# Modulation columns by halves, normalised rows on VectorE, a longer attention tail and separate buffers ahead of w3 in a memory-attention and MLP kernel

## The chip, the cores and the metric

The kernel runs on one core of one Trainium2 chip. The metric is the device time of one execution in microseconds (us). A comparison always uses runs of the kernel before on the same chip in the same rounds. "Ratio" below is the mean time of one kernel's fast runs over the mean of the other's of the same rounds, with a 95% interval; it is therefore not quite the ratio of the medians quoted beside it. Most experiments were timed in other rounds than the changed kernel, so a comparison with the changed kernel goes by the two ratios to the kernel before, or by medians where that is said, and is less certain. The engines are named as the profile names them: PE (TensorE matmuls), DVE (VectorE), ACT (ScalarE), POOL (GpSimd), SP (SyncE).

## The reference, cut to what matters

```python
mod = (silu(c) @ w_mod).reshape(1, 6, 1, 1024)          # sa, ca, ga, sb, cb, gb
h = layernorm(x) * (1 + ca) + sa                        # x: 1 x 2048 x 1024
x = x + ga * A(h, mem0, Wq, Wk, Wv, Wo, 32)   # 64 segments of 32 rows, 32 heads of 128,
                                              # 8 memory rows handed from segment to segment
h = layernorm(x) * (1 + cb) + sb
x = x + gb * B(h, w1, w2, w3, w4)
# B: h = gelu(layernorm(h0) @ w1); four column groups shifted by -1, +1, -2, +2 rows, then @ w2
#    x1 = h0 + that;  return x1 + gelu(layernorm(x1) @ w3) @ w4      (w3: 1024 -> 3584)
```

The stages that matter are, in order of time: the **opening** (modulation, first layer norm, first projections, to some 60 us), the **attention** (to some 760 us), the product with Wo (from 760 us), and the **passage** from w2 to w3 near 1100 us.

## The kernel before: the parts concerned

Opening. The weights of the modulation arrive in four pieces of 1 MB. Both vectors are written only when all four are in. The normalised tile `xn` is written by POOL.

```python
for q in range(4):
    wm = gchunk([P, KT, 512])
    last_wm = nc.sync.dma_start(wm[:], wslice(w_mod, q * 512, 512))
    wms.append(wm)
# ... (cut)
for half in range(2):
    for j in range(KT):
        for kt in range(KT):
            nc.tensor.matmul(pm[:, half * KT + j:half * KT + j + 1], lhsT=wms[half * 2 + j // 4][...], rhs=scT[:, kt:kt + 1], ...)
nc.vector.tensor_copy(saT[:], pm[:, 0:KT])
nc.vector.tensor_scalar(ca1T[:], pm[:, KT:2 * KT], 1.0, None, ALU.add)
# ... for each row tile (cut):
nc.vector.tensor_scalar(nm[:], mean, -1.0, None, ALU.mult)
nc.gpsimd.tensor_tensor(nmr[:], nm[:], rstd, ALU.mult)
nc.gpsimd.tensor_scalar(xn[:], xt[:], rstd, nmr[:], ALU.mult, ALU.add)
# then: transposes and segment sums of xn on PE; hh = xn^T * ca1T + saT
```

Attention. Heads are worked off between the projections of later heads; a tail of 1.55 heads is kept for afterwards.

```python
done, ahead = 0, len(att) - int(len(att) * 1.55 / H)
```

Passage. In w2 each row tile `t` goes through PE, then DVE (`x1b`, with a row sum), ACT (`Square`), POOL (three small instructions), ACT again (`Identity`, which writes the normalised `z`), and a DMA transposes `z` into z2a (tiles 0 to 7) or z2b (tiles 8 to 15). w3 is computed by a scheme with fewer products, which needs sums of z2a (`zs`) and of the weights (`ring`). For w3 a PSUM bank is copied by ACT (`snap`), added to another by DVE (`join`) and passed through gelu by ACT (`hq`).

```python
tp = LT2.enter_context(tc.tile_pool(name="x2_t", bufs=4))     # u2, x1b and z
# ... w2, tile t (cut):
    if i == 10:
        zu = z_sums(0) + w3_sums(0)
    if i >= 10:
        for f in zu[2 * (i - 10):2 * (i - 9)]:
            keep_order(f())
# ... then, over the memory that w2's pools have left (cut):
stm = RF.enter_context(tc.tile_pool(name="x3_sm", bufs=4, side="right"))    # the joins
# ...
def join(a, f, q, bank, s):
    t = stm.tile([P, 512], F32, name="join")
    nc.vector.tensor_tensor(t[:], st[q][bank][:], st[q][s][:], ALU.add)
    gelu(a, f, q, t)
```

## Time and profile before

| | kernel before |
|---|---|
| time, median of 4 runs | 1481.55 us (1480.31 to 1482.04) |
| span of the profiled execution, mean granted clock | 1480.2 us, 0.995 |
| PE busy | 1419.7 us, 96% |
| first projection on PE | 25.18 us |
| PE waits for the transposed V | 6.1 us |
| end of w2's last matmul, first matmul of w3 | 1116.91, 1119.07 us |

PE bounds this kernel, so it is read from PE's gaps: a change that removes no matmul can win only there, or where the granted clock is low. The prediction below shows the lines for that. Two further lines of the timeline of ACT in the kernel before; the columns are start, duration, engine, line and operation, and in brackets the idle time before it with what ended it.

```profile
1125.33 0.19 ACT L1147 ACTIVATION_READ_ACCUMULATOR z<-x1b,ln_nm 128x1 f32 x1
1126.72 1.24 ACT L1154 ACTIVATE z<-x1b,ln_nmr,ln_rstd 128x1024 bf16<-128x1024 f32 x1 [0.74 <-POOL ln_nmr L1153]
```

This is the last row tile of w2. ACT finishes its last normalise at 1127.96 us, 11.05 us after PE ended w2.

### The profile page before, as it was taken

How to read it: one execution, taken by the hardware profiler on the slowest of the kernel's cores; microseconds unless marked ns; L12 is line 12 of the kernel's file. 1: busy time of each engine (PE TensorE's matmuls, PEld its weight loads, DVE VectorE, ACT ScalarE, POOL GpSimd, SP SyncE). 2: the span in 40 equal slices, each digit the busy share in tenths (PEclk: the TensorE clock that was granted, in tenths of full speed). 3: DMA queues.
4: the chain of work that ended last, by engine and by line, in shares of the span. 5: the costliest groups of instructions: out<-in, count | busy, mean ns of one | idle time of the engine just before them, and what ended most of it. 6: DMA issues, size and time to landing. Idle time of an engine off the chain costs nothing.

```text
span 1480.2 us, 24704 instructions
## 1 busy us (share of the span) xinstructions
PE 1419.7 (96%) x9198; PEld 751.7 (51%) x9254; DVE 885.5 (60%) x1943; ACT 683.0 (46%) x1439; POOL 365.3 (25%) x526
## 2 busy tenths in 40 slices
PE   5999999999999999999998999999997999999998
PEld 3575555555565555555554444444443444444443
DVE  5526676777677777666652345345254657576684
ACT  2726666655665666665551122024465661046400
POOL 8411100000000001000001313213023653545625
PEclk9999999999999999999999999999998999999999
DMA  9678877787767887767579999985499783478812
GB/s 324 213 265 188 195 150 170 185 190 155 177 156 175 175 185 171 159 158 178 117 197 314 361 307 368 321 192 157 139 272 247 233 278 111 126 241 252 283 40 78
DMA packets 404149, 303.48 MB, mean 205 GB/s; under 512 B 199082, under 2 KB 356778, under 8 KB 402226
## 3 DMA queue, kind: packets, MB, share of 16 engines
q1 hardware_dynamic: 365904, 242.06, 61.7%
q10 hardware_dynamic: 29330, 30.89, 6.9%
q0 software_dynamic: 8784, 28.85, 6.6%
q8 instruction: 74, 1.21, 0.3%
q14 instruction: 57, 0.47, 0.1%
HBM read 200.56 MB, written 50.63 MB: 170 GB/s over the span
## 4 chain that ended last, share of the span: by engine, by line
PE 77%; DMA 7%; DVE 5%; ACT 4%; issue 4%; POOL 3%; ACTq 0%; SPq 0%; DVEq 0%; POOLq 0%
PE acc L620 30%; PE acc L902 7%; PE bank_b L1291 7%; PE bank_b L1240 6%; PE acc L1069 4%; PE acc L328 3%; PE bank_d L1240 3%; PE acc L318 3%; PE bank_e L1291 2%; PE bank_d L1291 2%; PE acc L1167 2%; PE ps_o L731 2%; PE ps_s L714 2%; PE bank_e L1240 1%; DMA V<-VT 1%
## 5 line engine op out<-in xcount | busy, mean ns | idle before, releaser
L902 PE MATMUL acc<-wstream,OTc 128*128 128x512 bf16 x940 | 207.8, 379 | 6.6 <-DMA OTc<-OTx_d 2.5
L620 PEld LDWEIGHTS <-T 128*128 128x128 f16 x1408 | 130.5, 97 | 119.6 <-issue 2.0
L588 ACT COPY snap<-acc 128x480 f32<-128x480 f32 x264 | 146.0, 564 | 89.2 <-PE acc L620 82.2
L620 PE MATMUL acc<-hh,T 128*128 128x480 bf16 (+1 forms) x704 | 163.1, 366 | 0.3 <-DVE VT L592 0.3
L620 PE MATMUL acc<-hs,T 128*128 128x480 f16 x704 | 157.1, 366 | 0.7 <-ACT snap L588 0.6
L902 PEld LDWEIGHTS <-OTc 128*128 128x128 bf16 x960 | 93.2, 98 | 117.7 <-issue 3.5
L1240 PEld LDWEIGHTS <-ring 128*128 128x128 f16 (+1 forms) x784 | 77.4, 99 | 109.7 <-issue 19.9
L756 POOL DMA_DIRECT2D OTx_d<-OT x32 | 24.9, 777 | 434.4 <-DMA OT<-O 341.6
L718 ACT ACTIVATE E<-ps_s 99x495 bf16<-99x495 f32 (+2 forms) x160 | 87.3, 546 | 48.2 <-PE ps_s L714 47.7
L620 PE MATMUL acc<-hh,wq 128*128 128x480 bf16 x464 | 103.9, 366 | 0.0
L738 DVE TENSOR_TENSOR O<-ps_o,rin_all 99x384 bf16<-99x384 f32 (+1 forms) x192 | 97.1, 509 | 3.8
L1205 ACT COPY snap<-bank_b 128x512 f32<-128x512 f32 x72 | 41.8, 586 | 105.6 <-PE bank_b L1291 58.2
L1291 PEld LDWEIGHTS <-hq 128*128 128x128 bf16 (+1 forms) x560 | 54.7, 98 | 66.1
L731 PE MATMUL ps_o<-V,E 99*128 99x129 bf16 (+1 forms) x704 | 79.7, 220 | 8.7 <-DMA V<-VT 6.1
L592 DVE TENSOR_TENSOR KT<-acc,snap 128x480 bf16<-128x480 f32 x116 | 74.9, 655 | 21.3 <-PE acc L620 18.9
L1095 DVE TENSOR_TENSOR ring<-ring 128x1024 f16<-128x1024 bf16 (+1 forms) x64 | 79.5, 1262 | 5.7 <-PE bank_b L1291 5.3
L731 PEld LDWEIGHTS <-E 99*128 99x128 bf16 (+1 forms) x704 | 56.2, 98 | 46.3 <-issue 8.8
L1010 ACT ACTIVATE u<-x,ln_nmr,ln_rstd 128x1024 bf16<-128x1024 f32 x16 | 19.7, 1231 | 127.0 <-DVE ln_nmr L1009 72.2
L720 DVE TENSOR_TENSOR E<-E,maskB 99x495 bf16<-99x495 bf16 (+1 forms) x128 | 48.1, 376 | 49.7 <-ACT E L718 47.7
L1244 ACT ACTIVATE hq<-join 128x512 bf16<-128x512 f32 x84 | 52.8, 630 | 47.0 <-DVE join L1248 47.0
L1291 PE MATMUL bank_b<-ring,hq 128*128 128x512 f16 (+1 forms) x334 | 73.1, 379 | 0.1
L592 DVE TENSOR_TENSOR VT<-acc,snap 128x480 bf16<-128x480 f32 x90 | 58.0, 651 | 24.9 <-PE acc L620 20.4
(242 smaller groups left out, 2509.5 us busy)
## 6 DMA issues: line engine op xcount, KB each, us to landing
wstream<-in_A_Wo_dram SPq DMA_DIRECT2D x31, 1024.0 KB, 11.1
OTx_d<-OT POOLq DMA_DIRECT2D x32, 512.0 KB, 7.2
wstream<-in_B_w_dram SPq DMA_DIRECT2D x28, 512.0 KB, 5.4
OTc<-OTx_d SPq DMA_DIRECT2D x14, 1024.0 KB, 8.7
ring<-in_B_w_dram SPq DMA_DIRECT2D x28, 512.0 KB, 6.5
ring<-in_B_w_dram SPq DMA_DIRECT2D x8, 1792.0 KB, 10.4
wq<-in_A_Wq_dram SPq DMA_DIRECT2D x16, 512.0 KB, 5.3
wk<-in_A_Wk_dram SPq DMA_DIRECT2D x16, 512.0 KB, 7.3
```

The costliest lines, as they stand in the source:

```text
L588: nc.scalar.copy(t[:], st[q][bank][:, 0:CH])
L592: nc.vector.tensor_tensor(view(d, i), chunks(st[q][bank]), chunks(st[q][s_]), ALU.add)
L620: nc.tensor.matmul(acc[:, 0:CH], lhsT=B[:, k, :], rhs=A[:, k, :], start=(j in (1, 2, 5) and k == 0), stop=(k == 3), skip_group_check=True)
L718: nc.scalar.activation(E[:rows, 0:o], ps[:rows, 0:o], ACT.Exp, scale=DH ** -0.5)
L731: nc.tensor.matmul(ps[:, i, :], lhsT=state["e", h, t // 5][:k, c:c + P], rhs=V[:k, t, 0:DH + 1], start=True, stop=True)
L738: nc.vector.tensor_tensor(O[:rows, ts[0]:ts[0] + n, :], ps[:rows, 0:n, 0:DH], rin[:, :, None].to_broadcast([rows, n, DH]), ALU.mult)
L902: mm = nc.tensor.matmul(accs[tt][:], lhsT=ot[hl // 4][:, hl % 4, tt * P:(tt + 1) * P], rhs=woc[hl // 4][:, hl % 4, :], start=(h == 0), sto ...
L1069: nc.tensor.matmul(acc[:], lhsT=w1s[:, kt, ct * P:(ct + 1) * P], rhs=zT[:, kt, b * 512:(b + 1) * 512], start=(kt == 0), stop=(kt == KT - 1))
L1095: return nc.vector.tensor_tensor(dst, a, b, op)
L1240: nc.tensor.matmul(acc[:], lhsT=B[:, k, q * P:(q + 1) * P], rhs=A[:, k, :], start=(start and k == 0), stop=(k == 3), skip_group_check=True)
L1244: nc.scalar.activation(hq[a][f][:, g * 2 + q, :], src[:], ACT.Gelu_apprx_tanh)
L1291: nc.tensor.matmul(acc[:], lhsT=L3[:, k, i * P:(i + 1) * P], rhs=R3[:, k, :], start=(start and k == 0), stop=(k == 13), skip_group_check=True)
```

## The change

It has four intentions: let the first rows be normalised and modulated before all modulation weights are in; take the normalised tile off POOL; give the attention more distance from its projections; and let w3 start without waiting for the last transposes of w2. The diff, cut to its core:

```diff
-            last_wm = nc.sync.dma_start(wm[:], wslice(w_mod, q * 512, 512))
+            last_wm = nc.sync.dma_start(wm[:], wslice(w_mod, q % 2 * D + q // 2 * 512, 512))
...
-        nc.vector.tensor_copy(saT[:], pm[:, 0:KT])
-        nc.vector.tensor_scalar(ca1T[:], pm[:, KT:2 * KT], 1.0, None, ALU.add)
+            cols = slice(q // 2 * 4, q // 2 * 4 + 4)
+            if q % 2:
+                nc.vector.tensor_scalar(ca1T[:, cols], pm[:, KT + cols.start:KT + cols.stop], 1.0, None, ALU.add)
+            else:
+                nc.vector.tensor_copy(saT[:, cols], pm[:, cols])
...
-                    nc.gpsimd.tensor_tensor(nmr[:], nm[:], rstd, ALU.mult)
-                    nc.gpsimd.tensor_scalar(xn[:], xt[:], rstd, nmr[:], ALU.mult, ALU.add)
+                    nc.vector.tensor_scalar(xn[:], xt[:], mean, rstd, ALU.subtract, ALU.mult)
...
-        done, ahead = 0, len(att) - int(len(att) * 1.55 / H)
+        done, ahead = 0, len(att) - int(len(att) * 1.75 / H)
...
+        tz = LT2.enter_context(tc.tile_pool(name="x2_z", bufs=4))
         tp = LT2.enter_context(tc.tile_pool(name="x2_t", bufs=4))
+        tu = LT2.enter_context(tc.tile_pool(name="x2_u", bufs=3))
...
-            if i == 10:
-                zu = z_sums(0) + w3_sums(0)
-            if i >= 10:
-                for f in zu[2 * (i - 10):2 * (i - 9)]:
-                    keep_order(f())
+            if i == 6:
+                zu = w3_sums(0) + [lambda: None] + z_sums(0)
+            if 6 <= i < 14 and i != 9:
+                keep_order(zu[i - 6]())
...
-        stm = RF.enter_context(tc.tile_pool(name="x3_sm", bufs=4, side="right"))
+        stm = RF.enter_context(tc.tile_pool(name="x3_sm", bufs=3, side="right"))
```

More of the change, by code (lines that the diff above doesn't have):

```diff
@@ L385, in first_pass @@
         pm = small_ps[:, 0:2 * KT]
-        for half in range(2):
-            for j in range(KT):
+        for q in range(4):
+            for j in range(4):
+                col = q % 2 * KT + q // 2 * 4 + j
                 for kt in range(KT):
-                    nc.tensor.matmul(pm[:, half * KT + j:half * KT + j + 1], lhsT=wms[half * 2 + j // 4][:, kt, (j % 4) * P:(j % 4 + 1) * P], rhs=scT[:, kt:kt + 1],
-                                     start=(kt == 0), stop=(kt == KT - 1))
-        nc.vector.tensor_copy(saT[:], pm[:, 0:KT])
-        nc.vector.tensor_scalar(ca1T[:], pm[:, KT:2 * KT], 1.0, None, ALU.add)
+                    nc.tensor.matmul(pm[:, col:col + 1], lhsT=wms[q][:, kt, j * P:(j + 1) * P], rhs=scT[:, kt:kt + 1], start=(kt == 0), stop=(kt == KT - 1))
+            cols = slice(q // 2 * 4, q // 2 * 4 + 4)
[3 more added lines that the diff above has]
+                nc.vector.tensor_copy(saT[:, cols], pm[:, cols])
         hsum = ps1.tile([P, KT, NSEG], F32, name="small_ps")
@@ L413, in f @@
                     mean, rstd = layernorm_stats(sm, xt[:])
-                    nm = sm.tile([P, 1], F32, name="ln_nm")
-                    nc.vector.tensor_scalar(nm[:], mean, -1.0, None, ALU.mult)
-                    nmr = sm.tile([P, 1], F32, name="ln_nmr")
-                    nc.gpsimd.tensor_tensor(nmr[:], nm[:], rstd, ALU.mult)
                     xn = xnp.tile([P, D], BF16, name="xn")
-                    nc.gpsimd.tensor_scalar(xn[:], xt[:], rstd, nmr[:], ALU.mult, ALU.add)
+                    nc.vector.tensor_scalar(xn[:], xt[:], mean, rstd, ALU.subtract, ALU.mult)
                     if t + 8 < NTT:
@@ L1158, in f @@
                 ts = slice(t * P, (t + 1) * P)
-                u = tp.tile([P, D], BF16, name="u2")
+                u = tu.tile([P, D], BF16, name="u2")
                 nc.sync.dma_start(u[:], u_d[ts, :])
@@ L1170, in f @@
                 nc.scalar.dma_start(x1b_d[ts, :], x1b[:])
-                zs[t] = z = tp.tile([P, D], BF16, name="z")
+                zs[t] = z = tz.tile([P, D], BF16, name="z")
                 ln_sums(bsm, z[:], x1b[:], sums)
```

## The prediction

> **What bounds the kernel now.** I read the page first, then the table of stretches of 20 us, then the waits of PE, then the timelines of single engines where PE had gaps.
>
> ```profile
> PE 1419.7 (96%) x9198; PEld 751.7 (51%) x9254; DVE 885.5 (60%) x1943; ACT 683.0 (46%) x1439; POOL 365.3 (25%) x526
> ```
>
> PE is busy for 1419.7 of 1480.2 us, so at most 60.5 us of gaps can be won, plus whatever PE runs at a low clock. The change removes no matmul. Its worth is therefore read only from the stretches in which PE has gaps.
>
> ```profile
> 0.00:20.00 20.00, 7.03 (x162) 6.43 (x163) 7.19 (x31) 1.46 (x2) 15.71 (x50) 1.00 0.97 320
> 20.00:40.00 20.00, 15.16 (x150) 8.77 (x149) 13.91 (x48) 9.86 (x21) 16.92 (x34) 1.00 1.04 338
> 700.00:720.00 20.00, 17.52 (x127) 10.04 (x126) 13.12 (x37) 11.17 (x26) 0.68 (x3) 1.00 0.68 121
> 1100.00:1120.00 20.00, 17.73 (x82) 7.93 (x83) 14.89 (x41) 10.63 (x15) 5.49 (x15) 1.00 0.94 239
> 1120.00:1140.00 20.00, 12.79 (x41) 4.72 (x40) 3.27 (x5) 10.58 (x17) 5.44 (x10) 0.67 0.99 227
> ```
>
> After each stretch and its length stand the busy times of PE, PEld, DVE, ACT and POOL, then the granted clock and the DMA share. Three places have gaps and are touched: the opening (13.0 + 4.8 us), the late attention, and the passage from w2 to w3 (2.3 + 7.2 us, the latter at a granted clock of 0.67). The waits of PE name the causes:
>
> ```profile
> PE bank_b L1240 <- ACT snap L1205: 10.3, 4, 5.8
> PE small_ps L389 <- DMA wchunk<-in_w_mod_dram: 9.3, 3, 6.1
> PE ps_o L731 <- DMA V<-VT: 6.1, 4, 2.3
> PE pt L423 <- POOL xn L419: 6.0, 6, 2.8
> ```
>
> In the opening, the chain that ended last goes through POOL, which has mask work queued between the third and the fourth normalised tile:
>
> ```profile
> 14.48 3.53 POOL xn L419 x3
> ...
> 22.41 1.19 POOL xn L419
> ...
> 25.18 6.08 PE acc L318 x23
> ```
>
> At the passage to w3, the timelines of DVE (two lines) and PE show a vector engine that twice stood for a DMA transpose, and PE behind it:
>
> ```profile
> 1104.39 1.24 DVE L1095 TENSOR_TENSOR zs<-z2a 128x2048 f16<-128x2048 bf16 x1 [3.57 <-DMA z2a<-z]
> ...
> 1131.84 1.29 DVE L1248 TENSOR_TENSOR join<-bank_e,snap 128x512 f32<-128x512 f32 x2 [12.53 <-DMA z2b<-z]
> ```
>
> ```profile
> 1119.07 2.67 PE L1240 MATMUL bank_b<-z2a,ring 128*128 128x512 bf16 x8 [2.17 <-POOL ln_ve L1149]
> ...
> 1135.29 3.57 PE L1240 MATMUL bank_b<-zs,ring 128*128 128x512 f16 x8 [5.78 <-ACT snap L1205]
> ```
>
> The join reads nothing of z2b. In the built program its four buffers lie at bytes 118752 to 126944 of a partition, and the four z buffers of the normalised w2 rows at 119616 to 127808: the join waited until the last transposes had read what it overwrites.
>
> **What the Trainium skill says.** "VectorE: DVE Perf Modes", section "The perf-mode tier table": a tensor_scalar with bf16 in SBUF runs at 4x, fp32 at 2x. The trace has no such bf16 instruction, but its fp32 `low<-rin_all` 128x704 took 527 ns, and the page's terms (704/2 + 158 cycles at 0.96 GHz) give 531, so it agrees; for the new 128x1024 the page gives (1024/4 + 158)/0.96 = 431 ns, an estimate. "GPSIMD Engine Reference", section "Specifications": POOL shares its SBUF interfaces with DVE. The trace agrees once: an `ln_rstd` of POOL took 1.40 us instead of 0.55 while a DVE sum ran. "TensorE: Matmul & The Clock Gate", section "Part 1: The HAM clock gate": an idle PE falls to half clock and comes back after some 3.4 us. After the 5.78 us wait, 8 matmuls took from 1135.29 to 1138.66 (0.42 us each) where the steady pitch is 0.216, which agrees. "DMA: Bandwidth & Descriptors", section "Issuing engines are not separate DMA queues": loads of all issuers interleave; shares of 0.97 and 1.04 in the first 40 us fit.
>
> **The change, part by part.**
>
> Opening. The four 1 MB pieces of w_mod are loaded as (shift, scale) for the first half of the columns, then for the second. PE starts on them at 10.29, 12.80, 15.51 and 18.30, and the transfers, not their order, set these times, so the last half is no earlier. What moves is the normalised tile: 1193 ns on POOL plus two little instructions become about 0.43 us on DVE, and the masks no longer stand in front. In the built order DVE writes tiles 0 and 1 behind the first half of the scale (about 14 us), tile 2 behind the third piece (16.6), four of the eight output rows of pair 0 (17.6 to 19.0), then after the fourth piece (19.4) tile 3 at about 20.0. Eight transposes (1.0) and the first output row (0.4) follow, so PE starts on the projections near 21.2 instead of 25.18: 4.0 us. From there to 50 us PE waited another 0.37 + 1.00 + 0.32 + 0.88 + 0.62 = 3.2 us for POOL. DVE now needs per pair of tiles four statistics of 0.6, two tiles of 0.43, one output row of 0.33 and little things, about 4.1 us, against 6.2 us of PE (24 matmuls at 0.203 plus transposes and sums), so it keeps up. But the DMA share is full to 57 us and everything is wanted earlier; I take back 0.7. Opening: 6.5 us.
>
> Attention. The tail kept for later grows from 1.55 to 1.75 heads, so heads run more slowly against the projections: 30.25 instead of 30.45 heads over 15 rounds. At the end of these rounds the lag is 0.2 heads of some 20 us, that is 4 us. The transposed V that PE waits for is issued by the projections, so the waits of 2.27 (ending at 715.03) and 1.55 us (760.57) and one smaller late one should go; the early one, 1.3 us before 130, has almost no new lag and stays. About 4.0 us. The extra attention in the tail is 0.2 x 2.3 us of PE work and covers little of the two waits for Wo loads (2.52 and 2.44): 0.3.
>
> w2 to w3. z now lies at 95040 to 103232, and the three joins at 120800 to 126944 lie over u2 alone, which DVE itself reads last; the built join carries no DMA wait. The sums of w3 stand earlier (tiles 6 to 8), but the first sum of z stays behind tile 10 and still needs the transposes of tile 7, which stand behind a u2 load that waits for tile 9 in both orders. So I expect the 3.57 us stand at 1104 to remain. After it, tile 11 goes first instead of sharing DVE with a sum: the last normalise on ACT ends about 1.35 us sooner, at 1126.6. DVE frees the last bank 1.1 us sooner. Then snap 0.5, join 0.7, gelu 0.6 and three snaps of 0.5 lead to PE resuming near 1130.0 instead of 1135.29: 5.3 us. PE's idle time shrinks to about 2 us, below what sent it to half clock; before, the 16 matmuls after it took 6.01 us instead of 3.46, and I count 1.0 of these 2.55. Together 6.3 us.
>
> Sum: 6.5 + 4.0 + 0.3 + 6.3 = 17.1; 1481.4 - 17.1 gives 1464.3, said as 1464.5.
>
> **The rivals.**
>
> First, DMA binds the opening. Shares of 0.97 and 1.04 speak for it: x tiles are asked for earlier, now against the same weights, and second-pair weights may come too late. Against it, the 19 MB moved by 57 us hold six 1 MB pieces of Wv that PE does not use before 68. Then the opening gives 4 and the whole 1467.
>
> Second, a new wait takes the place of the join's. ACT is in order: its last normalise stands between the two first snaps, so the ACT chain of 3.58 us per tile (PE: 3.45) binds w3's first group. It is in my sum. If the smaller rotation of u2 (3 instead of 4) also delays loads, the passage gives only 3 and the whole is 1468. The other way: if the first sum no longer stands for tile 7's transposes, the ACT chain ends up to 3.3 us sooner and PE gains some 3 more: 1461.5.
>
> Third, the shift of attention gives nothing: it reorders ACT and DVE in all fifteen rounds, and V waits can turn up elsewhere, since the odd heads' transposes follow attention. PE is at 19.6 to 20.0 of 20 us through most rounds, so there is little to win besides the three waits, and some to lose: 1469.
>
> Fourth, faster by over 2% needs 29.6 us, half of all PE gaps, among them the first 10 us of loads that nobody shortens. Unlikely.
>
> **Range and chances.** Two of three parts failing at once gives about 1472, all three over my sums about 1457. I say 1464.5 us, range 1457 to 1472.5; faster by over 2%: 0.03, within 2%: 0.96, slower: 0.01.
>
> **What would show each step right or wrong.** First projections on PE at 20.5 to 22 us and no wait for xn over 0.5 us; xn on DVE at 0.40 to 0.47 us. PE's wait for V at most 2 us in total, none after 600. The first join of w3 without a DMA wait, the stand of DVE for z2a still about 3.5 us, PE's longest wait for a snap about 2 us, and the granted clock in that stretch near 1. I am wrong if the opening gains under 3 us because PE then waits for x or weights, or if the passage still holds a wait over 4 us under another name.

## The result, and the profile after

The changed kernel took 1466.28 us (median of 4, 1465.43 to 1469.71) against 1481.55 us. The ratio is 0.9903 (0.9885 to 0.9920): about 1% faster, within the 2% called the same.

The first lines are the engines' line of the page of the changed kernel, then its table of stretches, with the same columns as in the prediction.

```profile
PE 1421.2 (97%) x9254; PEld 752.2 (51%) x9254; DVE 897.9 (61%) x1945; ACT 683.3 (47%) x1439; POOL 347.5 (24%) x494
```

```profile
0.00:20.00 20.00, 7.96 (x189) 7.51 (x190) 10.60 (x37) 2.81 (x5) 16.65 (x56) 1.00 0.98 328
20.00:40.00 20.00, 19.47 (x176) 10.91 (x174) 17.97 (x48) 13.46 (x30) 7.76 (x14) 0.91 1.08 349
700.00:720.00 20.00, 19.80 (x137) 11.27 (x136) 13.63 (x37) 13.00 (x30) 1.25 (x4) 1.00 0.70 143
1100.00:1120.00 20.00, 13.59 (x54) 5.36 (x53) 5.91 (x16) 13.08 (x20) 3.84 (x12) 0.85 1.12 255
1120.00:1140.00 20.00, 20.00 (x85) 8.61 (x84) 13.81 (x17) 11.99 (x21) 13.12 (x12) 0.90 0.84 252
```

PE is now nearly full from 20 to 40 us and at 700 us. The passage has moved into 1100 to 1120 and still holds 6.4 us of gaps and a clock of 0.85. The waits of PE in the changed kernel (total, count, longest) show which names went:

```profile
PE bank_b L1240 <- ACT snap L1205: 7.5, 5, 1.9
...
PE acc L901 <- DMA OTc<-OTx_d: 3.6, 2, 2.5
PE acc L901 <- DMA wstream<-in_A_Wo_dram: 2.5, 1, 2.5
```

The wait for `xn`, 6.0 us before, is down to one of 0.35, and the one for V from 6.1 to 1.3. The wait for the snap fell from 10.3 to 7.5, its longest from 5.8 to 1.9. The opening in the changed kernel, DVE (first two lines) and PE:

```profile
18.45 0.16 DVE L393 TENSOR_SCALAR ca1T<-small_ps 128x4 f32<-128x4 f32 x1 [0.31 <-PE small_ps L390]
19.14 0.57 DVE L418 TENSOR_SCALAR xn<-xt,ln_mv,ln_rstd 128x1024 bf16<-128x1024 bf16 x1 [0.25 <-PE small_ps L426]
```

```profile
14.87 2.72 PE L422 MATMUL pt<-ident,xn 128*128 128x128 bf16 x24
17.38 1.03 PE L390 MATMUL small_ps<-scT,wchunk 128*128 128x1 bf16 x32
...
20.89 0.77 PE L318 MATMUL acc<-hh,wq 128*128 128x480 bf16 x3 [0.32 <-DVE hh L435]
```

The first projection starts 3.5 us after PE begins on the fourth piece of weights (6.9 us in the kernel before, 18.30 to 25.18). This mark flatters the change: here 24 transposes stand on PE ahead of the fourth piece, with no wait between, where the kernel before has 16 and its weight load then still waits 0.31 us for the DMA. For the third piece PE waits for the DMA in both kernels; from that piece (13.99, and 15.51 before) the first projection comes after 6.9 us instead of 9.7.

In the passage PE takes up the matmuls `bank_b<-zs` of w3's first group in three goes, of 4, 4 and 8; below, their starts are its first, second and third return. The passage in the changed kernel, DVE first, then ACT, then PE:

```profile
1091.02 1.23 DVE L1094 TENSOR_TENSOR zs<-z2a 128x2048 f16<-128x2048 bf16 x1 [3.45 <-DMA z2a<-z]
...
1104.07 0.69 DVE L1170 SCALAR_TENSOR_TENSOR x1b<-acc,u 128x512 f32<-128x512 f32 x1 [1.54 <-DMA u<-u_d]
...
1114.84 1.29 DVE L1248 TENSOR_TENSOR join<-bank_e,snap 128x512 f32<-128x512 f32 x2 [9.00 <-ACT z L1155]
```

```profile
1107.53 1.15 ACT L1148 ACTIVATE z<-x1b,ln_nm 128x1024 bf16<-128x1024 f32 x1 [0.86 <-DMA z2b<-z]
...
1113.57 1.24 ACT L1155 ACTIVATE z<-x1b,ln_nmr,ln_rstd 128x1024 bf16<-128x1024 f32 x1 [0.74 <-POOL ln_nmr L1154]
```

```profile
1112.87 1.02 PE L1240 MATMUL bank_b<-zs,ring 128*128 128x512 f16 x4 [1.94 <-ACT snap L1205]
1115.33 1.86 PE L1240 MATMUL bank_b<-zs,ring 128*128 128x512 f16 x4 [1.43 <-ACT snap L1205]
1118.29 3.57 PE L1240 MATMUL bank_b<-zs,ring 128*128 128x512 f16 x8 [1.10 <-ACT snap L1205]
```

The 12.53 us for z2b ahead of the first join are gone, and PE's waits of 1.43 and 5.78 us before its second and third return have become three of 1.94, 1.43 and 1.10. But DVE now stands for a load of `u`, which it did not before. The last normalise ends at 1114.81, 11.15 us after w2's end (1103.66): no sooner than the 11.05 of before. And the 16 matmuls from 1118.29 still took 6.31 us, at half clock.

To see where time went I cut each profiled execution at three points of PE's timeline: the start of the last group of segment sums of `xn` (opening), the end of w2's last matmul (middle), and the start of w3's second group `bank_b<-z2a` (passage). Here are all fourteen profiles, in us; the last column is the gap time of PE from 300 to 760 us (460 minus PE's busy time there, or the sum of its parts).

| kernel | opening | middle | passage | rest | PE gaps 300 to 760 |
|---|---|---|---|---|---|
| before | 62.4 | 1054.5 | 24.4 | 338.9 | 7.5 |
| after | 54.9 | 1048.8 | 20.9 | 339.0 | 1.8 |
| e_open | 55.8 | 1055.2 | 24.0 | 339.4 | 7.2 |
| e_ahead | 61.5 | 1052.4 | 23.7 | 339.4 | 1.6 |
| e_pools | 62.2 | 1055.3 | 18.9 | 340.2 | 6.1 |
| e_sums | 62.1 | 1053.6 | 22.2 | 338.9 | 7.5 |
| e_xnpool | 61.6 | 1047.8 | 20.7 | 339.3 | 1.6 |
| e_whole | 58.9 | 1049.1 | 21.0 | 339.4 | 1.6 |
| e_tu4 | 54.9 | 1048.1 | 19.8 | 339.0 | 1.8 |
| e_zlate | 56.9 | 1050.3 | 17.4 | 339.1 | 1.7 |
| e_noahead | 56.7 | 1055.7 | 21.2 | 338.9 | 7.4 |
| e_oldsums | 56.2 | 1048.9 | 21.1 | 339.0 | 1.8 |
| e_dvenorm | 56.6 | 1049.5 | 17.1 | 339.1 | 1.7 |
| e_poolnorm | 56.5 | 1052.1 | 12.3 | 340.7 | 1.7 |

One profile is one execution, and columns differ by a us or two between executions of equal code. In these fourteen profiles PE began on the first modulation piece anywhere between 8.34 and 10.93 us, although no edit comes ahead of that load. The changed kernel's own profile had an early one (8.60 against 10.29 in the kernel before). So its opening, 7.5 us shorter, flatters the change. Over the eight profiles with the whole new opening the mean is 56.0, over the four with the whole old one 62.0: 6.0 us. From the third piece to the first projection these take 7.3 and 10.0 us on the mean. The passage takes 24.0 on the mean of the three profiles in which it is that of before, and 21.0 in the four in which it is that of the change (after, e_xnpool, e_whole, e_noahead): 3.1 us, a little less than the pair before and after shows.

### The profile page after: what moved, and what is told of

It reads as the page before. It is cut to its first block, busy times and chain, and to the rows that moved or that the text cites. A ratio compares the mean times of both kernels' runs of the same rounds, so it can differ in the third digit from the quotient of the medians.

```text
span 1463.6 us, 24731 instructions
## 1 busy us (share of the span) xinstructions
PE 1421.2 (97%) x9254; PEld 752.2 (51%) x9254; DVE 897.9 (61%) x1945; ACT 683.3 (47%) x1439; POOL 347.5 (24%) x494
## 3 DMA queue, kind: packets, MB, share of 16 engines
q8 instruction: 74, 1.21, 0.4%
## 4 chain that ended last, share of the span: by engine, by line
PE 80%; DMA 10%; issue 3%; DVE 3%; ACT 3%; POOL 1%; SPq 0%; ACTq 0%; DVEq 0%; POOLq 0%
PE acc L619 31%; PE acc L901 7%; PE bank_b L1291 7%; PE bank_b L1240 6%; PE acc L1068 4%; PE acc L328 4%; PE bank_d L1240 3%; PE acc L318 3%; PE bank_d L1291 2%; PE bank_e L1291 2%; PE ps_o L730 2%; PE ps_s L713 2%; PE acc L1168 2%; PE bank_e L1240 1%; DMA xt<-in_A_x_dram 1%
## 5 line engine op out<-in xcount | busy, mean ns | idle before, releaser
L591 DVE TENSOR_TENSOR KT<-acc,snap 128x480 bf16<-128x480 f32 x116 | 75.1, 655 | 19.8 <-PE acc L619 13.6
L591 DVE TENSOR_TENSOR VT<-acc,snap 128x480 bf16<-128x480 f32 x90 | 58.0, 651 | 18.7 <-PE acc L619 14.6
```

Of the source, the lines that this page charges most:

```text
L591: nc.vector.tensor_tensor(view(d, i), chunks(st[q][bank]), chunks(st[q][s_]), ALU.add)
```

## The experiments

My theory was that the parts add, each in its own stretch, and that in the passage the pools do the work. The rivals were that a gain is given back elsewhere, that the attention shift gives nothing by itself, and that in the passage a new wait takes the old one's place. First come four parts alone, on the kernel before.

### e_open: the opening alone

Edit: the first three hunks of the diff (load order, halves, `xn` on VectorE) on the kernel before.

> The kernel before with the opening of the change alone. Theory (the parts add, each in its own stretch): the last transposes of the opening ran 7.5 us earlier in the changed kernel, so this kernel is 7 to 8 us under the kernel before; its first projections start at 20.9 us, as in the changed kernel, and its late waits for V and its passage to w3 stay as before. Rival (what is won at the opening is given back later, when attention meets the same loads): under 4 us.

Measured: 1475.37 us against 1480.60, ratio 0.9958 (0.9946 to 0.9971), that is 6.2 us (4.3 to 8.0). The opening stretch is 55.8 against 62.4 and the passage as before (24.0). The first projection came at 22.69, not 20.9: its fourth piece was taken up at 18.77, so it came 3.9 us after that piece. The gain is kept to the end; the 7 to 8 us were read from the lucky profile, and 6 is the size.

### e_ahead: the attention tail alone

```diff
-        done, ahead = 0, len(att) - int(len(att) * 1.55 / H)
+        done, ahead = 0, len(att) - int(len(att) * 1.75 / H)
```

> The kernel before with the longer attention tail alone (1.75 heads for 1.55). Theory: the waits of PE for the transposed V fall from 6.1 us to about 1.3, the kernel is 4 to 5.5 us under the kernel before. Rival (reordering sixteen rounds of attention brings nothing by itself, and the waits for V went because the opening shifted projections against attention): under 1.5 us, waits for V still 5 us or more.

Measured: 1477.71 us, ratio 0.9975 (0.9957 to 0.9993), 3.7 us, with runs from 1472.70 to 1482.09. The wait for V, from the waits of PE in this kernel:

```profile
PE ps_o L731 <- DMA V<-VT: 1.3, 1, 1.3
```

This is the 1.3 us that was foretold, so the rival that the opening did it is refuted. The time is just under the expectation of 4 to 5.5 us, and its interval is wide; the counterpart e_noahead below sizes it better.

### e_pools: the pools alone

Edit: `z` and `u2` in pools of their own (4 and 3 buffers), three join buffers; the sums stay two per tile after tiles 10 to 13.

> The kernel before with the separate pools for z and u2 and three join buffers alone; the sums stay two per tile. Theory (the join's wait for the transposes of the last tiles was what counted): the first join has no DMA wait, PE comes back to w3 sooner, 3 to 4 us under the kernel before. Rival (the sums had to be spread as well, otherwise DVE and ACT reach the last tile later and the wait only changes its name): under 1.5 us.

Measured: 1476.00 us, ratio 0.9967 (0.9954 to 0.9979), 4.9 us. Line numbers are two higher here. DVE's first join, then two returns of PE:

```profile
1129.47 1.29 DVE L1250 TENSOR_TENSOR join<-bank_e,snap 128x512 f32<-128x512 f32 x2 [9.79 <-ACT z L1156]
```

```profile
1132.92 1.89 PE L1242 MATMUL bank_b<-zs,ring 128*128 128x512 f16 x8 [1.94 <-ACT snap L1207]
...
1146.27 1.89 PE L1242 MATMUL bank_b<-zs,ring 128*128 128x512 f16 x8 [1.09 <-ACT snap L1207]
```

There is no DMA wait at the join, and the passage is 18.9 us instead of 24.4. A wait of 1.09 us that the kernel before lacks gives some of it back later. The theory holds and the rival is refuted, but the gain is over the 3 to 4 us expected. The last normalise ends 12.0 us after w2, 0.9 later than in the kernel before: ACT waits 1.00 us for a transpose of `z`, which it did not there.

### e_sums: the spread sums alone

Edit: only the order of the sums (weights after tiles 6 to 8, z after 10 to 13), with the old pools.

> The kernel before with the spread sums alone; the joins still lie over z. Theory (the join waits for the transposes however early DVE is): the first join keeps a DMA wait of some 12 us and the kernel is within 0.7 us of the kernel before. Rival (the spread sums give the gain of the passage): 2 to 3.5 us under it.

Measured: 1479.67 us, ratio 1.0001 (0.9986 to 1.0015): nothing. The first join still stands:

```profile
1129.24 1.29 DVE L1247 TENSOR_TENSOR join<-bank_e,snap 128x512 f32<-128x512 f32 x2 [12.32 <-DMA z2b<-z]
```

By the time, the gain of the passage comes from the pools. The profile shows a little more: the last normalise ends 10.3 us after w2 instead of 11.05, and the passage is 22.2 us instead of 24.0 on the mean of before, but this one profile had a time like the others'. The three estimates add to 6.2 + 3.7 + 4.9 = 14.8 us; the whole change gives 14.4 by its ratio (0.0097 of 1481.55). Next come undone parts of the changed kernel.

### e_xnpool: the normalised tile back on POOL

```diff
-                    nc.vector.tensor_scalar(xn[:], xt[:], mean, rstd, ALU.subtract, ALU.mult)
+                    nc.vector.tensor_scalar(nm[:], mean, -1.0, None, ALU.mult)
+                    nc.gpsimd.tensor_tensor(nmr[:], nm[:], rstd, ALU.mult)
+                    nc.gpsimd.tensor_scalar(xn[:], xt[:], rstd, nmr[:], ALU.mult, ALU.add)
```

> The changed kernel with the normalised tile back on POOL; the halves of the modulation stay. Theory (the work taken from POOL and its queue of masks is what the opening gained): PE again waits some 6 us for xn, first projections near 25 us, the kernel is 5 to 7 us over the changed kernel. Rival (the halves gave the earlier start): first projections before 22.5 us and under 3 us lost.

Measured: 1473.57 us against 1481.18, ratio 0.9965 (0.9943 to 0.9986). By the medians it is 7.3 us over the changed kernel, by the ratios 9.2, with wide intervals; the opening stretch alone says 5.6 (61.6 against 56.0). The wait is back under its old name:

```profile
PE pt L426 <- POOL xn L422: 6.7, 6, 3.3
```

The first projection is at 24.37 us, 7.3 us after the fourth piece. With `xn` on POOL the halves gain nothing.

### e_whole: the modulation whole again

Edit: the old load order, `saT` and `ca1T` written whole after the fourth piece; `xn` stays on VectorE.

> The changed kernel with the modulation loaded as before (both halves of shift first, then of scale, columns written whole); the normalised tile stays on DVE. Theory (the fourth piece of the weights sets the start whichever order they have): first projections within 0.8 us of 20.9, the kernel is within 1.0 us of the changed kernel. Rival (without the halves all eight output rows of the first pair stand behind the last piece, 2.6 us of DVE): first projections at 22.5 us or later, 1.5 to 3 us over the changed kernel.

Measured: 1468.91 us, ratio 0.9912 (0.9899 to 0.9925), 1.3 us behind the changed kernel by the ratios, though the intervals overlap. The first projection is 4.9 us after the fourth piece (19.73 to 24.65) against 3.5 to 4.0 with the halves, because PE then waits for the fourth tile, which DVE writes at 22.52, behind both vectors (20.81) and four output rows (21.16 to 22.60):

```profile
23.11 1.03 PE L419 MATMUL pt<-ident,xn 128*128 128x128 bf16 x8 [1.14 <-DVE xn L415]
```

The result lies between the two expectations: the halves are worth about 1 us, and only together with `xn` on VectorE.

### e_noahead: the old attention tail in the changed kernel

Edit: 1.75 back to 1.55.

> The changed kernel with the attention tail of before (1.55 heads for 1.75). Theory (the gaps of PE between 300 and 760 us, 7.5 us in the kernel before and 1.9 in the changed one, come from heads that are too close behind their projections): these gaps are again 6 to 8 us and the kernel is 4 to 6.5 us over the changed kernel (ratio to the kernel before 0.9935 to 0.9950). Rival (the earlier opening alone removes them): gaps under 3 us, within 1.5 us of the changed kernel.

Measured: 1472.81 us against 1480.52, ratio 0.9937 (0.9922 to 0.9952), about 5 us over the changed kernel (0.0034 of 1481). The gaps from 300 to 760 us, the table of stretches of this kernel and of the changed one:

```profile
300.00:760.00 460.00, 452.65 (x3329) 265.44 (x3327) 321.89 (x834) 281.29 (x670) 33.55 (x96) 1.00 0.74 167
```

```profile
300.00:760.00 460.00, 458.17 (x3413) 270.03 (x3410) 325.99 (x846) 284.32 (x682) 34.57 (x100) 1.00 0.74 169
```

PE works 5.5 us more in the same 460 us when the tail is longer. Every profile with 1.75 has 1.6 to 1.8 us of gaps there, every one with 1.55 has 6.1 to 7.5. The effect is shown.

### e_oldsums: the old order of the sums in the changed kernel

Edit: the sums again two per tile after tiles 10 to 13, z first; the pools as changed.

> The changed kernel with the sums of before (two per tile after tiles 10 to 13), pools as changed. Theory A (the spread sums are worth nothing: the pools alone took 5.5 us from the stretch between the end of w2 and the second product of w3, pools and spread sums together 3.4): within 1.5 us of the changed kernel, on either side, that stretch 19 to 21 us. Theory B (the spread was needed, as the change meant it): 2 us or more over the changed kernel, that stretch 22.5 us or more.

Measured: 1466.25 us, ratio 0.9919 (0.9894 to 0.9944). By the medians that is level with the changed kernel, by the ratios 2.4 us over it, with an interval of 3.7 us either way, so the time decides little; the passage is 21.1 against 20.9. Theory A is favoured: the spread is worth nothing that these runs can tell. Within the passage it does do what it was meant to do. Without it the last normalise ends 12.5 us after w2 and PE's third return comes 16.0 after, with it 11.15 and 14.6. But in the changed kernel the 16 matmuls after that return took 6.31 us, here 5.13, which took most of it back. The run also shows the noise of one profile: e_pools has the same pools and the same order of sums and passed in 18.9. In e_oldsums the first group of w3 and the group of the third return ran at half clock (3.49 and 3.57 us for 8 matmuls), in e_pools only the first two (2.35 and 3.15).

### e_tu4: four buffers of u2

```diff
-        tu = LT2.enter_context(tc.tile_pool(name="x2_u", bufs=3))
+        tu = LT2.enter_context(tc.tile_pool(name="x2_u", bufs=4))
```

> The changed kernel with four buffers of u2 for three; the joins still lie over u2 alone. Theory (the smaller rotation held back the last load of u2, DVE stood 1.5 us for it and the last normalise came late): the stand of DVE for u goes, the last normalise on ACT and PE's return come about 1.4 us sooner, 1 to 2 us under the changed kernel. Rival (the ACT chain of 3.58 us a tile sets the last normalise, not DVE): within 0.5 us.

Measured: 1467.24 us, ratio 0.9912 (0.9894 to 0.9930): by the time no gain. In the profile the stand of 1.54 us for `u` is gone, so is ACT's wait of 0.86 us for a transpose, w3's first matmul follows w2's end after 0.95 us instead of 1.93, and the last normalise ends 10.2 us after w2 instead of 11.15. The passage is 1.1 us shorter. That wait of ACT (0.65 to 1.31 us) is in every profile with three buffers of u2, apart from the two with the sums of z one tile later (e_zlate, e_dvenorm), and in none with four. So the mechanism is there at about 1 us, and with runs from 1463.53 to 1473.37 the timing can't show it. The join now has this line:

```profile
1111.20 0.69 DVE L1248 TENSOR_TENSOR join<-bank_e,snap 128x512 f32<-128x512 f32 x1 [7.06 <-ACT snap L1205]
```

In the changed kernel the first join waited for the last normalise (9.00 us, ACT z). With three u2 buffers the small statistics tiles lie at bytes 125760 to 127268 and so under a join buffer (120800 to 126944); with four they lie above it. By itself that wait cost little, since the second snap came from the same ACT just after.

### e_zlate: the sums of z one tile later

```diff
-            if 6 <= i < 14 and i != 9:
-                keep_order(zu[i - 6]())
+            if 6 <= i < 9:
+                keep_order(zu[i - 6]())
+            if 11 <= i < 15:
+                keep_order(zu[i - 8]())
```

> The changed kernel with the four sums of z one tile later (after tiles 11 to 14). Theory (DVE's stand of 3.45 us for the transposes of tile 7 makes ACT late, and ACT cannot catch up because it needs 3.58 us a tile against PE's 3.45): the stand falls under 0.7 us, the last normalise and PE's first return come 2.5 to 3.5 us sooner, 2 to 3 us under the changed kernel. Rival (ACT is bound by the transposes that free its z buffers and by the order of DMA, so the stand only moves on): within 0.7 us.

Measured: 1462.67 us against 1481.18, ratio 0.9882 (0.9867 to 0.9898), about 3.1 us under the changed kernel by the ratios, though the intervals overlap a little. The first sum of z on DVE no longer stands at all, and the last normalise ends 8.8 us after w2 instead of 11.15:

```profile
1094.61 1.23 DVE L1094 TENSOR_TENSOR zs<-z2a 128x2048 f16<-128x2048 bf16 x1
```

The passage is 17.4 us instead of 20.9. The stand of 3.45 us on DVE, which was no idle time of PE at all, had made ACT late, and ACT, at some 3.58 us a tile (Square 1.13, accumulator 0.19, wait for POOL 1.21, Identity 1.24, less overlaps), can't catch up with PE's 3.45.

### e_dvenorm: the last normalise on VectorE

Edit, on top of e_zlate (cut; `last` is tile 15):

```diff
+            if last:
+                nc.vector.tensor_scalar(dst, src, rstd[:], nmr[:], ALU.mult, ALU.add)
+            else:
                 nc.scalar.activation(dst, src, ACT.Identity, bias=nmr[:], scale=rstd[:])
```

> The kernel with the sums of z one tile later, and in it the last normalise (tile 15) written by VectorE instead of ScalarE. Theory (in order, ScalarE makes its first two snaps of w3 around the last normalise; 0.7 us of waiting for POOL and 1.24 us of work stand ahead of the second snap): PE's second and third return come 1.5 to 2 us sooner after the end of w2, the stretch from the end of w2 to the second product is 15.4 to 16.4 us instead of 17.4. Rival (the chain bank, snap, join, gelu of w3 itself sets these returns): the stretch stays 17 to 17.8 us.

Measured: 1464.20 us, ratio 0.9884 (0.9869 to 0.9898): level with e_zlate, passage 17.1. By the numbers the rival was right, but the lines say something else. DVE, then PE:

```profile
1113.71 0.81 DVE L1156 TENSOR_SCALAR z<-x1b,ln_rstd,ln_nmr 128x1024 bf16<-128x1024 f32 x1 [6.40 <-POOL ln_nmr L1154]
1114.65 1.29 DVE L1253 TENSOR_TENSOR join<-bank_e,snap 128x512 f32<-128x512 f32 x2
```

```profile
1118.11 2.52 PE L1245 MATMUL bank_b<-zs,ring 128*128 128x512 f16 x8 [3.20 <-ACT snap L1210]
```

The wait of 1.43 us between the two halves of a group went, but the normalise now stood ahead of the join on DVE, the gelu behind the join came late, and PE waited 3.20 us instead of 1.94. The wait only moved: 0.61 and 3.20 us here, 0.56, 1.43 and 1.94 in e_zlate.

### e_poolnorm: the last two normalises on POOL

Edit: e_zlate, with four buffers of u2, and the normalise of tiles 14 and 15 by `nc.gpsimd.tensor_scalar`.

> Sums of z one tile later, four buffers of u2, and the last two normalises (tiles 14 and 15) written by GpSimd, which is idle there; no vector work stands ahead of the first join, whose buffers lie over u2 alone. Theory (ScalarE in order was what PE's returns waited for; in the run with the last normalise on VectorE the gain was eaten because the join then stood behind it): the first snap comes about 1.3 us sooner and the first join at once after its snap, the stretch from the end of w2 to the second product is 14.5 to 16.3 us instead of 17.1 to 17.4, and the kernel is 1 to 2.5 us under the one with the later sums alone (ratio to the kernel before 0.9860 to 0.9880). Rival (bank, snap, join and gelu of w3 set the returns by themselves, or the clock takes it back): the stretch stays 17 us or more.

Measured: 1462.32 us against 1481.34, ratio 0.9872 (0.9856 to 0.9889), 19.0 us under the kernel before and about 4.6 under the changed one. DVE and PE at the passage, and PE later:

```profile
1112.90 1.29 DVE L1253 TENSOR_TENSOR join<-bank_e,snap 128x512 f32<-128x512 f32 x2 [3.18 <-ACT snap L1210]
```

```profile
1114.66 1.89 PE L1245 MATMUL bank_b<-zs,ring 128*128 128x512 f16 x8
1117.43 1.89 PE L1245 MATMUL bank_b<-zs,ring 128*128 128x512 f16 x8 [0.89 <-ACT snap L1210]
...
1142.59 1.89 PE L1245 MATMUL bank_b<-zs,ring 128*128 128x512 f16 x8 [0.80 <-ACT snap L1210]
...
1191.92 1.89 PE L1245 MATMUL bank_b<-zs,ring 128*128 128x512 f16 x8 [0.74 <-ACT snap L1210]
```

The passage is 12.3 us, less than any theory said, since no group ran at half clock: 8 matmuls took 1.89 each time. Against e_zlate two things were changed at once (ScalarE relieved of two normalises, four buffers of u2), but in e_zlate DVE no longer stood for `u` either, so I put the 5 us down to ScalarE working in order, and to the clock that stayed up because of it; how the 5 us divide between these two is open. The total is only 0.3 us under e_zlate's by the medians and 1.5 by the ratios, inside the intervals. Two new waits of 0.80 and 0.74 us later in w3 give 1.5 back, and this profile had 5.0 us of waits for loads of Wo, which e_zlate's had 2.7 of. It is the fastest version I ran, but whether it beats e_zlate isn't settled.

## Why the prediction was right, point by point

The total was right: 1464.5 us predicted, 1466.28 measured, inside 1457 to 1472.5. Its four terms were not all so good, and it was partly luck that their errors cancelled.

**Opening, 6.5 predicted.** e_open gives 6.2 and the stretches 6.0, and the rival that DMA binds it is refuted: it would have left 4. The first projection at 21.2 was met by 20.89 only because the pieces came early. Measured from the fourth piece it is 3.5 to 4.0 us where the working said 2.9, and the fourth piece itself was taken up 3.4 us after the third instead of 2.8, behind 24 transposes that the working did not count: the transfers alone do not set its time. One mis-sized term in it is `xn` on VectorE, "about 0.43 us", which took 0.551 on the mean of 16. From the third piece to the first projection the gain is 2.7 us where the working said 4.0; so about 3.3 of the 6.0 us come later, where it said 3.2 less 0.7. The two errors offset each other. That most of it is POOL's work and its queue, not the halves, is shown by e_xnpool and e_whole.

**Attention, 4.0 predicted.** The step was right and a little small: the gaps between 300 and 760 us fell by 5.6 us (7.5 to 1.8), and undoing it costs about 5. V waits fell by 4.8 in all, and none is left after 600 us. The third rival, that the shift gives nothing, is refuted by e_ahead and e_noahead together.

**Wo loads, 0.3 predicted.** Not decidable: the wait for `wstream` was 2.4 before and 2.5 after, while profiles of the same middle code had none to 5.0. Of the two waits that the prediction calls Wo loads, the one of 2.52 us was for attention's own output (`OTc<-OTx_d`).

**Passage, 6.3 predicted.** This is where the working failed; 3.5 came (24.4 to 20.9), 3.1 on the mean of several profiles. The failing step, as the prediction put it, is "the last normalise on ACT ends about 1.35 us sooner": it ended 11.15 us after w2's end instead of 11.05. A stand for a load of `u` (1.54 us) and one of ACT for a transpose (0.86) took it back. The working left out what three buffers of u2 cost: the spread sums bring the last normalise 0.8 us forward with the old pools (e_sums) and 1.35 with the new (e_oldsums against the changed kernel), the new pools alone put it 0.9 back (e_pools), and with four buffers of u2 it ends at 10.2 (e_tu4). Each is one profile, and e_pools and e_oldsums, with the same code here, differ by 0.5.

PE's third return came 3.75 us sooner relative to w2's end (18.38 before, 14.63 after), not 5.3. The steps from the last normalise to that return took 3.5 us, as the working has them (3.4), so 1.45 of the missing 1.55 is the normalise that ended 0.1 later instead of 1.35 sooner. The other failing term is "I count 1.0" for the clock. The 16 matmuls after the last return took 6.31 us against 6.01; so 3.75 less 0.3 gives the 3.45 measured. The sentence that PE's idle time would shrink to about 2 us and stay below what sent it to half clock did not hold: there were three waits of 1.94, 1.43 and 1.10 us, and half clock. Of the signs that the prediction names, two failed, `xn` at 0.40 to 0.47 us and a granted clock near 1 in that stretch (0.85 and 0.90); the others came. Its line that the three joins lie over u2 alone was wrong too: they reach over the small statistics as well (e_tu4), and the first join waited for the last normalise, at little cost.

The second rival's form, that the smaller rotation of u2 also delays loads and the passage gives only 3, is what happened, and e_tu4 shows the mechanism at about 1 us. Its other form, that ACT would be sooner if the first sum did not stand, was not in this change, but e_zlate made it so and got the 3 us named there. The second rival's core, that ACT's order sets PE's returns, is borne out by e_zlate and e_poolnorm. The predicted removal of the join's DMA wait, and its cause in shared addresses, is confirmed by e_pools against e_sums.

The sum came out because attention was undersized by 1 to 1.6 us and the passage oversized by 2.8 or more: 6.0 + 5.6 + 3.5 = 15.1 against 14.4 by the ratio.

## What to carry to other kernels

When a pool is opened over memory that an earlier stage leaves, ask for each new buffer who reads the old one last: here the answer was a DMA transpose, then the small statistics tiles, and the join itself read neither. An engine standing idle off the critical path can still set it: DVE's 3.45 us delayed ACT, which works in order and had no slack, and so PE; moving four instructions by one tile shortened the passage by 3.5 us (20.9 to 17.4), as much as the change's own rework of it (24.4 to 20.9). And take sizes from several profiles or from a point inside the profile that the change can't move (the third piece of weights), not from the absolute time of one execution, when loads at the start scatter by 2 us.

## What the Trainium skill lacked or had wrong

- "VectorE: DVE Perf Modes", the perf-mode tier table: its 4x terms gave 431 ns, an estimate, for a bf16 128x1024 `tensor_scalar` with two scalars per partition; the 16 in the changed kernel took 551 ns on the mean. The one fp32-to-bf16 `tensor_scalar` of e_dvenorm took 0.81 us, where the page's 2x terms give 698 ns as an estimate.
- "TensorE: Matmul & The Clock Gate", Part 1: it names an idle window of about 3.4 us that runs free. Here 16 matmuls at half clock (6.31 us) followed three waits of 1.94, 1.43 and 1.10 us with matmuls between them; in e_pools full clock followed waits of 1.04, 1.43 and 1.94 us, in e_poolnorm waits of 0.94 and 0.89. The page's remark that the count of slow matmuls varies from run to run, made for a kernel's start, agrees: the passage of the same code took 18.9 and 21.1 us (e_pools, e_oldsums). The page does say elsewhere that frequent short idles can bring the throttle about; what it lacks is how long they must be, and these runs do not settle that.
- "DMA: Bandwidth & Descriptors": it has no figure for the scatter of first arrivals. PE began on the first modulation piece between 8.34 and 10.93 us in fourteen profiles.
